# A new order of units, loads and stores for a grouped-query attention forward and backward kernel

## The chip, the cores and the metric

The kernel runs on one core of a Trainium2 chip. The metric is device time in microseconds (us), lower is better. Ratios are computed as the mean time of one kernel's fast runs over the mean of the other's fast runs of the same rounds, so they are not quite the ratio of the medians that are quoted beside them. "Span" is the length of the one profiled execution, some 1.8 to 2.2 us shorter than that execution's measured time.

## The reference

```python
B, Hq, Hkv, Sq, Sk, D = 32, 32, 4, 4, 2048, 128       # all bf16
def fwd(q, k, v):                                      # k, v repeated 8 times over the heads
    p = softmax(einsum("bhqd,bhkd->bhqk", q, k) * D ** -0.5)
    return einsum("bhqk,bhkd->bhqd", p, v)
out, vjp = jax.vjp(fwd, q, k, v)
return (out, *vjp(grad_out))                           # out, dq, dk, dv
```

Each of the 32 batches reads K and V (4 heads of 2048 rows) and writes dK and dV of the same size. Everything else is small.

## The kernel before

The program is a list of *units* written down offline as a string of four characters each: what to do, which part, where (PSUM bank, row slot or engine), which tile. Every engine works through its own units in the order of this list.

```python
SLOTS, E_TILES, DS_TILES = 20, 2, 2          # 20 row slots of 1 MB, shared by loads and outputs
PLAN = ("a000a110b120a030b040a150e400f4A0..." ...)   # [cut: 3232 units in all]

def emit(u):
    if name in ("LK", "LV"):                 # load K or V of a head pair: 1056 or 1024 KB
        for w in (slice(0, Sk), slice(Sk, n)) if b == 0 else (slice(0, n),):
            nc.sync.dma_start(out=x[:, w], in_=src[:, w])
    elif name in ("KT", "VT", "ET", "DT"):   # four transposes on TensorE into one PSUM bank
        ...
    elif name in ("O", "DQ"):                # 32 small matmuls for each half
        for c in range(8):
            for h, r in enumerate(rows):
                nc.tensor.matmul(t[name][r, :], lhsT=left[:, j, r, odd], rhs=right[:, 4 * i + j, :, odd], ...)
    elif name in ("DV", "DK"):               # two matmuls into two PSUM banks
        ...
    elif name in ("DVe", "DKe"):             # eviction of these two banks into an output slot
        copy = nc.scalar.copy if u.where == "A" else nc.vector.tensor_copy
        copy(out=heads_of(t[name[:2], "out", g])[:, :, QW * i:QW * i + QW],
             in_=t[name[:2], i, g].rearrange("p (h c) -> p h c", h=2))
    elif name in ("SV", "SK"):               # store dV or dK of a head pair: 1024 or 1056 KB
        nc.sync.dma_start(out=(dv_r if name == "SV" else dk_r)[i][b], in_=t["D" + name[1], "out", i][:, 0:n])
    # [cut: S, DP, softmax, DS, small units]

with tc.manual_schedule():
    for u in units:
        emit(u)
```

All loads and stores are issued by one engine, SP, in the order of the list. In a steady batch of about 101 units it issues LK0 SK1 SV1 LV0 SV0 LK1 SK0 LV1. One batch is 274 matmuls, each with a weight load of its own.

## Time and profile before

| before | |
|---|---|
| time, median of 4 runs | 671.61 us (671.47 to 672.95) |
| span of the profiled run | 671.1 us |
| bytes moved | 272.65 MB in 256 transfers of about 1 MB (the first four in two halves each) |
| PE, DVE, ACT busy | 91%, 85%, 85% |

The lines on which the reading rests are in the prediction below.

```profile
q8 instruction: 69, 1.13, 0.6%
...
out_dram<-row SPq DMA_DIRECT2D x64, 1024.0 KB, 20.4
```

The reader is to see that 69 packets of 16 KB are read as instructions while the kernel runs, and that a transfer that needs about 2.5 us by itself takes 20 us from issue to landing.

### The profile page before, as it was taken

How to read it: one execution, taken by the hardware profiler on the slowest of the kernel's cores; microseconds unless marked ns; L12 is line 12 of the kernel's file. 1: busy time of each engine (PE TensorE's matmuls, PEld its weight loads, DVE VectorE, ACT ScalarE, POOL GpSimd, SP SyncE). 2: the span in 40 equal slices, each digit the busy share in tenths (PEclk: the TensorE clock that was granted, in tenths of full speed). 3: DMA queues.
4: the chain of work that ended last, by engine and by line, in shares of the span. 5: the costliest groups of instructions: out<-in, count | busy, mean ns of one | idle time of the engine just before them, and what ended most of it. 6: DMA issues, size and time to landing. Idle time of an engine off the chain costs nothing.

```text
span 671.1 us, 20678 instructions
## 1 busy us (share of the span) xinstructions
PE 607.9 (91%) x8768; PEld 401.4 (60%) x8768; DVE 572.0 (85%) x736; ACT 569.6 (85%) x802; POOL 39.0 (6%) x102
## 2 busy tenths in 40 slices
PE   6998999999998999988998989988999989898993
PEld 5665566666665666655655655655655666565651
DVE  1988799999997999988888989887888979896994
ACT  4997899999997999888888989887888979886894
POOL 0000000000000000000000000000000000000000
PEclk9999999999998999999999999998999989998997
DMA  9999999999999999999999999999999999999867
GB/s 354 417 424 423 419 381 423 423 423 423 423 426 424 424 423 424 424 425 426 414 420 425 413 417 421 414 422 424 396 388 408 417 424 424 404 421 423 347 258 322
DMA packets 37533, 273.97 MB, mean 408 GB/s; under 512 B 4160, under 2 KB 4160, under 8 KB 5184
## 3 DMA queue, kind: packets, MB, share of 16 engines
q1 hardware_dynamic: 37440, 272.65, 98.2%
q8 instruction: 69, 1.13, 0.6%
q14 instruction: 24, 0.20, 0.1%
HBM read 136.31 MB, written 136.31 MB: 406 GB/s over the span
## 4 chain that ended last, share of the span: by engine, by line
DMA 50%; PE 37%; DVE 4%; ACT 4%; issue 3%; SPq 0%; POOL 0%; DVEq 0%; ACTq 0%; POOLq 0%
DMA row<-in_k_dram 50%; PE psum L241 19%; PE psum L310 8%; PE psum L288 5%; PE psum L255 5%; ACT row L316 3%; DVE vt_sb L209 2%; DVE ds_sb L303 1%; DVE row L316 0%; DVE e_sb L260 0%; ACT e_sb L264 0%; PE psum L230 0%; SPq L226 0%; ACT dt_sb L207 0%; DVE row L296 0%
## 5 line engine op out<-in xcount | busy, mean ns | idle before, releaser
L241 PE MATMUL psum<-ident,row 128*128 128x128 f32 x2048 | 290.1, 284 | 28.4 <-DMA row<-in_k_dram 21.5
L316 ACT CAST row<-psum 128x1024 bf16<-128x1024 f32 x292 | 289.2, 1023 | 30.9 <-PE psum L310 29.1
L241 PEld LDWEIGHTS psum<-ident,row 128*128 128x128 f32 x2048 | 224.7, 143 | 94.8 <-issue 32.0
L316 DVE CAST row<-psum 128x1024 bf16<-128x1024 f32 x220 | 264.9, 1217 | 5.7 <-PE psum L310 2.9
L207 ACT COPY kt_sb<-psum 128x512 f32<-128x512 f32 x190 | 110.2, 598 | 20.6 <-PE psum L241 20.4
L207 ACT COPY vt_sb<-psum 128x512 f32<-128x512 f32 x160 | 92.0, 602 | 35.3 <-PE psum L241 34.6
L303 DVE SCALAR_TENSOR_TENSOR ds_sb<-psum,delta,e_sb 128x1024 bf16<-128x1024 f32 x64 | 82.1, 1283 | 13.4 <-PE psum L255 9.0
L310 PE MATMUL psum<-ds_sb,qp_sb 32*128 32x512 bf16 x512 | 76.9, 383 | 3.4 <-ACT row L316 1.0
L260 DVE TENSOR_SCALAR_CACHE_REDUCE e_sb<-psum 128x2048 bf16<-128x2048 f32 x32 | 73.3, 2292 | 5.7 <-PE psum L255 5.7
L310 PE MATMUL psum<-e_sb,dop_sb 32*128 32x512 bf16 x512 | 68.8, 388 | 2.5 <-issue 1.0
L209 DVE COPY kt_sb<-psum 128x1024 bf16<-128x1024 bf16 x66 | 45.0, 685 | 28.4 <-PE psum L241 27.8
L209 DVE COPY vt_sb<-psum 128x1024 bf16<-128x1024 bf16 x96 | 60.7, 684 | 10.0 <-PE psum L241 9.8
L264 ACT ACTIVATE e_sb<-psum,m 128x2048 bf16<-128x2048 f32 x32 | 64.0, 2001 | 0.2 <-DVE e_sb L260 0.2
L271 POOL TENSOR_SCALAR dop_sb<-row,rinv 128x128 bf16<-128x128 bf16 x32 | 19.3, 603 | 605.3 <-DVE rinv L268 530.3
L241 PE MATMUL psum<-ident,ds_sb 128*128 128x128 f32 x256 | 41.8, 286 | 9.6 <-DVE vt_sb L209 7.0
L288 PE MATMUL psum<-row,dt_sb 128*32 128x128 bf16 x2048 | 43.5, 222 | 6.2 <-issue 5.6
L310 PEld LDWEIGHTS <-qp_sb 32*128 32x128 bf16 x512 | 19.4, 91 | 46.1 <-issue 42.6
L255 PE MATMUL psum<-vt_sb,qdt_sb 128*32 128x512 bf16 x512 | 40.7, 388 | 4.6 <-issue 4.5
L288 PEld LDWEIGHTS <-dt_sb 128*32 128x32 bf16 x2048 | 30.8, 95 | 22.0 <-issue 21.1
L241 PEld LDWEIGHTS psum<-ident,ds_sb 128*128 128x128 f32 x256 | 26.9, 140 | 27.2 <-DVE vt_sb L209 16.4
L207 ACT COPY dt_sb<-psum 128x512 f32<-128x512 f32 x63 | 38.4, 611 | 1.0 <-PE psum L241 0.9
L288 PEld LDWEIGHTS <-et_sb 128*32 128x32 bf16 x2048 | 30.4, 95 | 13.8 <-ACT et_sb L207 11.3
(29 smaller groups left out, 310.1 us busy)
## 6 DMA issues: line engine op xcount, KB each, us to landing
out_dram<-row SPq DMA_DIRECT2D x64, 1056.0 KB, 20.1
out_dram<-row SPq DMA_DIRECT2D x64, 1024.0 KB, 20.4
row<-in_k_dram SPq DMA_DIRECT2D x62, 1056.0 KB, 18.1
row<-in_v_dram SPq DMA_DIRECT2D x62, 1024.0 KB, 20.5
row<-in_v_dram SPq DMA_DIRECT2D x4, 512.0 KB, 9.4
row<-in_k_dram SPq DMA_DIRECT2D x2, 544.0 KB, 5.3
row<-in_k_dram SPq DMA_DIRECT2D x2, 512.0 KB, 4.4
```

The lines of the kernel that those rows point to most:

```text
L207: nc.scalar.copy(out=out.bitcast(FP32), in_=in_)
L209: nc.vector.tensor_copy(out=out, in_=in_.bitcast(BF16))
L241: nc.tensor.transpose(out=ps[:, P * j:P * j + P], in_=src[:, 4 * half + j, :], identity=ident32[:])
L255: nc.tensor.matmul(out[r, QW * w:QW * w + QW], lhsT=t["qdt"][:, P * side + 32 * h:P * side + 32 * h + 32], rhs=t[x, NH * i + h][:, QW * w: ...
L260: nc.vector.tensor_scalar(out=t["e"][:], in0=t["S"], scalar1=-scale, scalar2=None, op0=ALU.mult, op1=ALU.min, accum_out=t["m"][:])
L264: nc.scalar.activation(out=t["e"][:], in_=t["S"], func=ACT.Exp, bias=t["m"][:], scale=scale, accum_out=t["l"][:])
L271: nc.gpsimd.tensor_scalar(out=t["dop"][:], in0=t["go"], scalar1=t["rinv"][:], scalar2=None, op0=ALU.mult)
L288: nc.tensor.matmul(t[name][r, :], lhsT=left[:, j, r, odd], rhs=right[:, 4 * i + j, :, odd], start=(i == 0 and c == 0), stop=(i == 1 and c ...
L303: nc.vector.scalar_tensor_tensor(out=t["ds"][:, w], in0=t["DP", i], scalar=t["dl"][:], in1=t["e"][:, w], op0=ALU.subtract, op1=ALU.mult)
L310: nc.tensor.matmul(acc[:, QW * (h % 2):QW * (h % 2) + QW], lhsT=t[still][rows[h], :], rhs=t[moving][rows[h], QW * i:QW * i + QW], start=Tr ...
L316: copy(out=heads_of(t[name[:2], "out", g])[:, :, QW * i:QW * i + QW], in_=t[name[:2], i, g].rearrange("p (h c) -> p h c", h=2))
```

## The change

The intent: batch the loads and the stores (SP now issues SV0 SK0 SV1 SK1 and LK0 LV1 LK1 LV0 in a steady batch), give output slots at the first write, have the last load land earlier so that more stores lie behind it, warm the array up before the first data, and shorten the last drain with half-size stores. The whole string of units is new, with other positions of nearly all units, other PSUM banks, and other choices of ACT or DVE for the evictions.

```diff
+LAST = 31
+WARM_UP = 20
 PLAN = (
-    # [cut: 3232 units of before]
+    # [cut: 3236 units of after]
-            T[u.b]["D" + u.name[1], "out", u.part] = slots[int(u.where, 36)]
+            T[u.b]["D" + u.name[1], "out", u.part % 2] = slots[int(u.where, 36)]
-            for w in (slice(0, Sk), slice(Sk, n)) if b == 0 else (slice(0, n),):
-                nc.sync.dma_start(out=x[:, w], in_=src[:, w])
+            nc.sync.dma_start(out=x[:, 0:n], in_=src)
-            copy(out=heads_of(t[name[:2], "out", g])[:, :, QW * i:QW * i + QW],
-                 in_=t[name[:2], i, g].rearrange("p (h c) -> p h c", h=2))
+            copy(out=t[name[:2], "out", g][:, 2 * QW * i:2 * QW * i + 2 * QW], in_=t[name[:2], i, g])
+            half, g = divmod(i, 2)
+            w = (slice(0, n), slice(0, ROW // 2), slice(ROW // 2, n))[half]
+            nc.sync.dma_start(out=(...)[g][b][:, w], in_=t["D" + name[1], "out", g][:, w])
     with tc.manual_schedule():
+        for _ in range(WARM_UP):
+            nc.tensor.transpose(out=psum[:, QW * (BANKS - 1):QW * (BANKS - 1) + P], in_=ident32[:], identity=ident32[:])
```

## The prediction

> **What bounds the kernel now.** I read the page first: the busy table, the slices, the DMA part, the chain. PE is busy 91% of the span and DVE and ACT 85%, so no compute engine is full. The DMA lines are.
>
> ```profile
> DMA  9999999999999999999999999999999999999867
> GB/s 354 417 424 423 419 381 423 423 423 423 423 426 424 424 423 424 424 425 426 414 420 425 413 417 421 414 422 424 396 388 408 417 424 424 404 421 423 347 258 322
> ...
> q1 hardware_dynamic: 37440, 272.65, 98.2%
> ...
> DMA 50%; PE 37%; DVE 4%; ACT 4%; issue 3%; SPq 0%; POOL 0%; DVEq 0%; ACTq 0%; POOLq 0%
> DMA row<-in_k_dram 50%; PE psum L241 19%; PE psum L310 8%; PE psum L288 5%; PE psum L255 5%; ACT row L316 3%; DVE vt_sb L209 2%; DVE ds_sb L303 1%; DVE row L316 0%; DVE e_sb L260 0%; ACT e_sb L264 0%; PE psum L230 0%; SPq L226 0%; ACT dt_sb L207 0%; DVE row L296 0%
> ```
>
> To see here: the DMA engines are full up to slice 37, at 424 GB/s in the good slices. They move 272.65 MB; at 424 GB/s that alone is 643 us of the 671. The chain puts 50% on DMA; its PE part lies in the first 255 us, where DMA and PE are both nearly full.
>
> So the question is where the other 28 us are. The stretches view splits the span (columns: stretch, length, busy us and instructions of PE, PEld, DVE, ACT, POOL, granted clock, DMA share, GB/s):
>
> ```profile
> 0.00:34.00 34.00, 26.66 (x274) 19.96 (x275) 18.84 (x26) 22.81 (x34) 1.89 (x9) 1.00 0.96 387
> 34.00:104.00 70.00, 64.86 (x932) 42.68 (x931) 60.06 (x79) 60.16 (x84) 4.79 (x12) 0.98 1.01 411
> 104.00:248.00 144.00, 138.53 (x2040) 90.59 (x2038) 131.88 (x172) 129.64 (x185) 8.38 (x21) 0.99 1.01 424
> 248.00:328.00 80.00, 72.86 (x1084) 48.17 (x1083) 70.30 (x92) 69.23 (x99) 4.79 (x12) 1.00 1.01 424
> 328.00:472.00 144.00, 130.05 (x1907) 85.93 (x1906) 124.46 (x160) 121.97 (x174) 8.38 (x21) 0.99 1.01 419
> 472.00:624.00 152.00, 139.47 (x1979) 92.23 (x1977) 131.30 (x167) 129.86 (x185) 8.38 (x21) 0.98 1.01 412
> 624.00:664.00 40.00, 35.45 (x572) 21.85 (x568) 35.16 (x45) 35.89 (x48) 2.40 (x6) 1.00 0.76 313
> 664.00:671.10 7.10, 0.00 (x0) 0.00 (x0) 0.00 (x0) 0.00 (x0) 0.00 (x0) 0.50 0.56 231
> ```
>
> To see: three losses against 424. (a) The start: 387 in 34 us loses 34*(1-387/424) = 3.0 us. (b) Slow packets with DMA share 1.01, so no lack of work: 70*(1-411/424) = 2.1, 144*(1-419/424) = 1.7 and 152*(1-412/424) = 4.3, in sum 8.1 us. (c) The end: 40*(1-313/424) = 10.5 us, and 7.1*(1-231/424) = 3.2 us, of which 1.5 us is after the last packet (it ends at 669.55 by the packet records). In the end stretch the DMA share is 0.76, so the queue is empty: stores wait for compute. The three make 25 of the 28 us; the rest is in the rounding of 424. The queue's timeline shows it as one held-up row of eleven stores:
>
> ```profile
> 614.00 3.92 SPq L320 DMA_DIRECT2D out_dram<-row  x2
> 619.27 0.34 SPq L226 DMA_DIRECT2D row<-in_v_dram  x1
> 621.69 41.73 SPq L320 DMA_DIRECT2D out_dram<-row  x11
> ```
>
> The last load is issued at 619.3 and lands at 631.7 (landing records); eleven stores, 11*2.55 = 28 us of DMA work, then have to stretch over 38 us because batches 30 and 31 are still being computed.
>
> **What the Trainium skill says.** "DMA: Bandwidth & Descriptors", section Specifications, gives 16 DMA engines per core, a fabric ceiling of 435 GB/s and an HBM share of about 358 GB/s per core; "HBM Reference", section Specifications (TRN2), adds that a core streaming alone measures about 425 GB/s. This trace agrees with 425 (424 sustained), not with 358. So about 643 us plus the ends is a floor that no order of work can pass. The same page, section Rules for kernel authors, advises at least 1 MiB per DMA; the transfers here are 1024 and 1056 KB, so the half-size first loads and last stores are the only departures. "TensorE: Matmul & The Clock Gate", Part 1, says the array runs at half clock until about 3.4 us of activity. The start agrees: the first 16 transposes that ran together took 3.65 us (228 ns each), 16 later ones 1.90 us (119 ns).
>
> **The change part by part.**
> Bytes: none are removed. Still 256 transfers of full size, in four fewer first-load halves and four more last-store halves. Floor unchanged.
> Evictions: the strided two-head output copies become contiguous, x512 of them (ACT 1023 ns, DVE 1217 ns each); I expect at most a few tens of ns. By counts, ACT takes 345 of them (before 292) and gives up 108+28+28 copies of about 600 ns for 26 gained and 64 small ones: about -12 us of 570. DVE: -53*1.217, +108*0.685, +28*0.684, -26*0.692, +28*0.692, small ones -20: about +10 of 572. Both stay far below 640, so this is worth 0 by itself.
> Start: the first K rows come whole, so the second one lands at about 8.2 us as now and V follows it instead of coming between. The 20 warm-up transposes run from 1.6 us (identity ready) for about 20*0.228 = 4.6 us, until the first row is there, and save about 16*(228-119) = 1.7 us of PE. The first softmax can start about 3 us sooner (now 15.41). But the DMA queue is full with twelve loads (12*2.55 = 31 us) whatever PE does; worth 0 to 1 us.
> End: this is the real gain. In the new order the stores behind the last load are 11 of full size and 8 halves, 15 equivalents instead of 11. The last load therefore lands at about 631.7 - 4*2.55 = 621.5 us, and 15*2.55 = 38 us of stores lie beside the last 1.6 to 2 batches of compute (19 us of PE each: 608/32). PE needs, from the landing of the last load, about what it needs now, 631.7 to 663 = 31 us. So 38 us of DMA cover 31 us of compute plus the last eviction and half-size store. From loss (c), 12.2 us without the 1.5 us after the last packet, I keep 2 us for stores that come just in time: gain about 10 us. The halves cut the last drain from about 2.55 to 1.3 us; this is in that number.
> Middle: the slow packets of (b). By the landing records, eight transfers take 19.95 us at best and 20.4 on average. Within the good stretches a load after a store, a store after a load and two stores in a row all take 2.44 to 2.57 us by their size, so grouping by four has no turnaround to save. But slow packets are rarer when more transfers are in flight: about 10 ns excess per packet with four in flight, 6 with five, 3 with six (40 to 624 us). The new order issues four stores and two loads before a load must wait for the slot of the first of these stores, so five to six are in flight where now it is mostly four to five after 328 us. I expect about 4 of the 8 us back, with little confidence.
> Sum: 671.7 - 10 - 4 - 1 = about 656.5 us.
>
> **The rivals.**
> R1: only the end is gained and the slow packets stay. At the mean rate up to 624 us (416.4 GB/s from the stretches), 272.65/0.4164 = 655 us, plus 1.5 at the end and 2 of starvation and 0.6 between span and measured time: 659 us, 1.9% faster, "same". For it: the cause of slow packets isn't visible, and 104 to 328 us was free of them with the old order.
> R2: runs of four loads make more slow packets. In the old order the excess sits nearly all in the one place per batch where two loads follow each other (V1, K0) and the store before them. Three such places per batch could add 5 to 10 us: 664 us. Against it: the first twelve loads run in a row at 2.48 to 2.57 us each with one outlier of 3.70.
> R3: everything works and the middle runs at 424 throughout: 34 us at 387 (13.2 MB), then 259.5/0.424 = 612, plus 1.5, 2 and 0.6: 650 us.
> R4: compute becomes the bound. PE needs 19.0 us per batch, DMA 20.0. If slots given at first write make evictions wait for the landing of a store, or the moved copies make PE wait 1.5 us more per batch, the time stays at 665 to 672. PE at 138.5 of 144 us in the good stretch speaks for some risk, the DMA rate of 424 in that stretch against it.
>
> **Range and chances.** The 2% line is 658.2 us. R1 lies just above, my sum just below, R3 well below. Prediction 656.5 us, 8 in 10 between 648 and 665. Chances: faster 0.58, same 0.40, slower 0.02 (slower would need R2 and R4 together and lose the end as well).
>
> **What would show it.** In the changed profile: DMA digits of 9 to the last slice and no row of stores stretched beyond 2.6 us each (end gained); DMA share near 1 but GB/s of 410 to 419 in the middle (slow packets stay, R1, R2) or 424 (R3); the chain of waits on DMA nearly throughout. If the DMA share falls below 1 in the middle, or the output copies wait for stores in the list of waits, R4 is right and I am wrong. The start is right if the first softmax instruction begins near 12.5 us while the time gains at most 1 us from it.

## The result, and the profile after

After: 674.58 us median of 4 runs (673.12 to 675.51), before in the same rounds 671.61 us. The ratio is 1.0038 with a 95% interval of 1.0016 to 1.006: 0.4% slower, "same" by the 2% rule, and outside the predicted range of 648 to 665.

The page of the kernel after, its DMA slices, queues and chain:

```profile
DMA  8999999999999999999999999999999999999997
GB/s 363 408 420 427 407 400 415 410 424 425 424 424 423 424 424 424 423 419 416 406 394 424 424 419 419 400 407 418 408 404 408 403 414 357 423 425 354 378 395 309
...
q8 instruction: 69, 1.13, 0.6%
...
PE 43%; DMA 38%; ACT 11%; DVE 4%; issue 2%; SPq 0%; ACTq 0%; DVEq 0%
```

The end is filled as predicted: digits of 9 up to slice 39, where before had 8 and 6. But the GB/s line is lower in many other slices: by more than 3 in 17 of the 40, higher by as much in 10. The stretches view says the same (columns as in the prediction):

```profile
328.00:472.00 144.00, 135.78 (x1908) 90.06 (x1904) 125.80 (x164) 122.34 (x167) 8.43 (x21) 0.99 1.01 412
472.00:624.00 152.00, 142.24 (x2012) 93.25 (x1999) 134.45 (x176) 131.75 (x182) 8.43 (x21) 1.00 0.99 400
624.00:664.00 40.00, 37.16 (x580) 22.99 (x578) 32.80 (x41) 37.91 (x53) 2.42 (x6) 1.00 0.94 385
```

412 and 400 GB/s stand where before has 419 and 412, and 385 where before has 313. What was won at the end had been lost earlier. The chain is not on DMA nearly throughout, as the prediction wanted it: PE has 43% of it where before has 37%, DMA 38% where before has 50%. The waits of the queue that issues transfers (columns: us in total, times, longest) changed their kind. Before:

```profile
SPq L320 <- DMA out_dram<-row: 125.1, 64, 2.2
SPq L226 <- DMA out_dram<-row: 105.4, 23, 5.6
SPq L320 <- DVE row L316: 89.1, 15, 9.3
```

After:

```profile
SPq L324 <- ACT row L297: 193.9, 30, 9.2
SPq L229 <- DMA out_dram<-row: 115.2, 43, 10.6
SPq L324 <- DVE row L319: 85.3, 36, 11.3
SPq L324 <- ACT row L319: 64.1, 38, 6.6
```

Before, the queue mostly waits for landings; after, it mostly waits for an engine to fill a row (L297 is the dq or o row on ACT, L319 the output copies). And the evictions wait for stores, which never showed in before, in the waits of ACT:

```profile
ACT row L319 <- DMA out_dram<-row: 11.5, 12, 1.3
```

These are the signs that the prediction had named for its rival R4. They are true, but the experiments show that they are not the whole story.

**The view that decides.** I counted the transfers that have landed by a given time, from the trace's semaphore records: each transfer raises its semaphore sixteen times, once for each DMA engine, and it has landed at the last of the sixteen. So the count is that of the slowest engine. Halves count as half; the total is 256.

```text
landed by (us)    100   200   300   400   500   600   640
before             36    74   113   152   190   229   244
after              36    75   114   152   190   228   244
```

The two kernels land their transfers at the same pace, within one transfer, all the way to 640 us. At that point each has 12 left, about 30 us of work at 2.5 us each; before's last lands at 670.0 and after's at 671.7. So nothing that the new order does to compute, to the place of the last load or to the grouping changed the pace of the slowest engine, which decides when a transfer has landed. The question of the experiments is what sets that pace, as both are well above what 424 GB/s would give.

### The profile page after: what moved, and what is told of

Same layout as the page of the kernel before. It is cut to its first block, busy times and chain, and to the rows that moved or that the text cites. A ratio compares the mean times of both kernels' runs of the same rounds, so it can differ in the third digit from the quotient of the medians.

```text
span 672.8 us, 20669 instructions
## 1 busy us (share of the span) xinstructions
PE 624.8 (93%) x8788; PEld 413.9 (62%) x8788; DVE 580.1 (86%) x757; ACT 569.3 (85%) x781; POOL 39.2 (6%) x102
## 3 DMA queue, kind: packets, MB, share of 16 engines
q1 hardware_dynamic: 37440, 272.65, 98.7%
q8 instruction: 69, 1.13, 0.6%
## 4 chain that ended last, share of the span: by engine, by line
PE 43%; DMA 38%; ACT 11%; DVE 4%; issue 2%; SPq 0%; ACTq 0%; DVEq 0%
DMA out_dram<-row 28%; PE psum L244 21%; PE psum L313 10%; ACT row L319 6%; PE psum L291 6%; DMA row<-in_v_dram 6%; PE psum L258 5%; DMA row<-in_k_dram 5%; ACT kt_sb L212 2%; DVE row L319 2%; ACT row L297 1%; DVE vt_sb L214 1%; DVE ds_sb L306 1%; ACT vt_sb L212 1%; ACT e_sb L267 0%
## 5 line engine op out<-in xcount | busy, mean ns | idle before, releaser
L319 ACT CAST row<-psum 128x1024 bf16<-128x1024 f32 x345 | 341.0, 1027 | 43.0 <-PE psum L313 30.3
L319 DVE CAST row<-psum 128x1024 bf16<-128x1024 f32 x167 | 202.7, 1218 | 7.1 <-PE psum L313 5.5
L214 DVE COPY kt_sb<-psum 128x1024 bf16<-128x1024 bf16 x174 | 117.4, 688 | 33.8 <-PE psum L244 27.6
L313 PE MATMUL psum<-ds_sb,qp_sb 32*128 32x512 bf16 x512 | 94.2, 387 | 14.7 <-ACT row L319 10.1
L214 DVE COPY vt_sb<-psum 128x1024 bf16<-128x1024 bf16 x124 | 82.5, 686 | 11.8 <-PE psum L244 9.5
L313 PE MATMUL psum<-e_sb,dop_sb 32*128 32x512 bf16 x512 | 82.8, 381 | 5.1 <-ACT row L319 1.1
L212 ACT COPY vt_sb<-psum 128x512 f32<-128x512 f32 x132 | 75.8, 602 | 6.7 <-PE psum L244 6.5
L212 ACT COPY kt_sb<-psum 128x512 f32<-128x512 f32 x82 | 47.5, 593 | 22.0 <-PE psum L244 19.7
L313 PEld LDWEIGHTS <-dop_sb 32*128 32x128 bf16 x512 | 23.7, 91 | 41.1 <-issue 30.0
L258 PEld LDWEIGHTS <-qdt_sb 128*32 128x32 bf16 x1024 | 20.7, 95 | 27.3 <-issue 19.6
```

The lines of the kernel that those rows point to most:

```text
L212: nc.scalar.copy(out=out.bitcast(FP32), in_=in_)
L214: nc.vector.tensor_copy(out=out, in_=in_.bitcast(BF16))
L258: nc.tensor.matmul(out[r, QW * w:QW * w + QW], lhsT=t["qdt"][:, P * side + 32 * h:P * side + 32 * h + 32], rhs=t[x, NH * i + h][:, QW * w: ...
L313: nc.tensor.matmul(acc[:, QW * (h % 2):QW * (h % 2) + QW], lhsT=t[still][rows[h], :], rhs=t[moving][rows[h], QW * i:QW * i + QW], start=Tr ...
L319: copy(out=t[name[:2], "out", g][:, 2 * QW * i:2 * QW * i + 2 * QW], in_=t[name[:2], i, g])
```

## The experiments

Eighteen kernels ran. Where a median of before is given, it is of the same chip and rounds.

### Transfers alone and compute alone

Four kernels take each order apart: only its loads and stores, or all its compute with the transfers cut short from batch 4 on (512 columns; stores 512 columns throughout). All four give wrong results.

```diff
 # dma_before, dma_after [cut: the slots are set to zero first]
+            if u.name in ("LK", "LV", "SV", "SK"):
                 emit(u)
 # comp_before, comp_after
-                nc.sync.dma_start(out=x[:, 0:n], in_=src)  # comp_after; comp_before has the same cut in its loop
+                w = slice(0 if b < 4 else n - QW, n)       # and the last 512 columns of each store
+                nc.sync.dma_start(out=x[:, w], in_=src[:, w])
```

dma_before:

> The transfers of the kernel before alone, in its order and slots, without any compute (wrong results on purpose). In the profile of before one DMA engine lands each transfer up to 13 us after the first one, and late in the run the spread no longer grows: the slowest of the 16 engines seems to set 2.58 us per transfer. If that engine is slow by itself: 256*2.58 + 3 = about 663 us. If it is slow only because of what compute brings (instruction fetches, waits): about 647 us (424 GB/s all the way).

dma_after:

> The transfers of the changed kernel alone, in its order. Theory loop (a store's landing, an eviction into its slot and the next store follow each other in a circle): the order of transfers costs nothing by itself, so within 3 us of the transfers of before alone. Rival grouping (four loads in a row make slow packets): 5 us or more slower than them.

comp_before:

> The kernel before with all transfers from batch 4 on cut to 512 columns, all stores too (wrong results on purpose): what compute needs when transfers cost next to nothing. All theories: clearly below 671; from the stretch where PE was 96% busy I expect 600 to 640 us.

comp_after:

> The same cut in the changed kernel. Theory loop: compute alone is not what takes 20.8 us per batch; within 10 us of the kernel before with the same cut. Rival compute (the new order of units makes the engines themselves slower; PE busy rose from 608 to 625 us): 660 us or more, 20 us or more over the other.

Measured, beside 672.72 us for before: dma_before 647.38 us (ratio 0.9621), dma_after 649.15 (0.9653), comp_before 627.18 (0.9334), comp_after 652.41 (0.9698).

Grouping loads and stores costs the transfers alone 1.8 us, and the floor of about 647 us is real. But the new order makes compute alone 25 us slower. The busy time of PE grew by the same amount, and the weight loads wait for ACT's evictions of PSUM. First the busy line of comp_before's page, then one line of the waits of its weight loads:

```profile
PE 598.3 (96%) x8768; PEld 394.9 (63%) x8768; DVE 568.7 (91%) x736; ACT 566.2 (91%) x802; POOL 39.0 (6%) x102
```

```profile
PEld psum L241 <- ACT row L316: 10.5, 33, 0.4
```

The same two of comp_after:

```profile
PE 622.5 (96%) x8788; PEld 414.0 (64%) x8788; DVE 578.3 (89%) x757; ACT 568.1 (87%) x781; POOL 39.2 (6%) x102
```

```profile
PEld psum L245 <- ACT row L320: 28.0, 79, 0.6
```

PE is "96% busy" in both, for the same matmuls (8788 in comp_after are the 8768 plus the 20 of the warm-up). Matching every instruction record to its unit shows what the busy time hides: units whose first matmul starts 0.04 to 0.075 us after the eviction of their PSUM bank ends, having waited for it. Between batches 8 and 24 they are 6.0 per batch in comp_before and 7.9 in comp_after. Compared with the usual step from a unit of the kind before them, they come 1.85 and 2.66 us late in sum per batch. The time of a batch (here and below the mean distance between the starts of the first dq matmuls, DQ, of successive batches) is 18.9 us in comp_before and 19.8 us in comp_after, so these waits could account for 0.8 of the 0.9 us. That the bank waits make this difference is read from the records; no run took them away by themselves.

This cannot be all, though. The larger of the two bounds is 647 us for before and 652 for after, and both kernels are 22 to 24 us above it.

### What do the transfers lose when compute runs beside them?

In dma_before the landings of one transfer on its sixteen engines, from first to last, spread over 2.7 us at the most. In before the spread grows: 7.7 us at 198 us (times here are those of the first landing), 12.5 us at 400, and one engine stays about 13 us late until the last load, while the second slowest is 5 to 6 us late. A difference between these two programs that the page shows is the instruction queue q8: before has 69 such packets, dma_before none. (A smaller instruction queue, q14, has 24 packets of 0.20 MB in sum in before, and 2 in dma_before and dma_pe. No run tests it.) The next runs put a bare instruction stream beside the transfers, small matmuls on a constant, without any data in common. (Wrong results.)

```diff
 # dma_pe; dma_pe_after is the same on after's transfers with 8788 matmuls
+        for j in range(8768):
+            nc.tensor.matmul(psum[:, QW * (j % BANKS):QW * (j % BANKS) + 104], lhsT=ident[:], rhs=ident[:, 0:104], ...)
 # dma_pe_half: half as many, twice as wide
+        for j in range(4384):
+            nc.tensor.matmul(psum[:, ... + 208], lhsT=ident[:], rhs=wide[:, 0:208], ...)
```

dma_pe:

> Transfers only in the order of before (647.4 us when run alone), and beside them 8768 small matmuls without any data in common with the transfers, so that the instruction stream of TensorE is as long as in the kernel before. Wrong on purpose. Theory fetch (instruction fetches ride the same 16 engines, and each costs the engine that carries it about 1.4 us): some 60 to 70 fetches appear, the landings of one transfer spread over more than 4 us, and the time rises by 4 to 12 us, to 651 to 659. Rival (the lag comes from what the engines read and write in SBUF): 646 to 649, and the spread stays below 3 us.

Measured: 666.48 us (666.38 to 666.64), beside 671.88 for before: 19 us over the transfers alone, more than the 4 to 12 that I had expected, with 68 fetches. The spread of landings is 10.3 us at 196 us and 13.5 at 403, as in before.

dma_pe_half:

> As the run of the transfers of before beside 8768 small matmuls (666.5 us), but with 4384 matmuls of twice the columns: the same busy time of TensorE, half the instructions. Wrong on purpose. Theory fetch (what delays the transfers is that the instruction stream is read by the same 16 engines): the 19 us over the transfers alone halve, to 655 to 659, with some 34 fetches. Rival (TensorE's own reads and writes slow the transfers): 664 to 668.

Measured: 656.21 us, with 34 fetches. TensorE was busy 393.5 us, beside 411.7 in dma_pe. Half the instructions, about half the loss (8.8 of 19.1 us) at nearly the same busy time: the loss goes with the number of instructions and not with the busy time of TensorE. The weight loads halve too, so their reads alone aren't set apart by this run.

The GB/s and queue lines of dma_before:

```profile
GB/s 332 426 427 424 424 419 427 427 425 427 427 424 425 426 428 428 428 427 428 427 427 428 427 428 427 426 428 428 428 429 427 427 428 427 428 429 427 427 428 346
...
q1 hardware_dynamic: 37440, 272.65, 100.4%
```

The same of dma_pe:

```profile
GB/s 349 420 422 423 422 423 423 423 422 423 423 425 421 422 423 420 409 398 398 420 421 395 420 395 422 420 419 413 428 427 427 428 426 426 429 425 428 427 428 164
...
q1 hardware_dynamic: 37440, 272.65, 98.7%
q8 instruction: 68, 1.11, 0.6%
```

And the instruction queue of dma_pe_half:

```profile
q8 instruction: 34, 0.56, 0.3%
```

To see: a queue that takes 0.6% of the engines' time costs 3% of the kernel's. The rate dips only a little while TensorE runs (to slice 26); the last slice of dma_pe, 164 GB/s, is mostly the backlog of the late engine, which the others don't help with. In the records of before a fetch takes about 0.94 us. A data packet that starts as it ends, so presumably on the same engine, takes 0.7 to 0.85 us instead of 0.31 (66 of the 69 fetches have one): about 1.4 us of one engine for each fetch. The trace does not name the engine of a packet, so how the fetches are shared out can't be read from it.

Carrying the fetches is not all of the 19.1 us, though. The packet records give this account of the loss of the slowest engine over dma_before (the last column is what the first three leave of the measured loss, so an estimate):

```text
us, mean of 16 engines   fetches and the   other slow   slowest engine
                         packets after     packets      beyond the mean
dma_pe, 19.1             5.9               5.8          7.5
dma_pe_half, 8.8         3.0               -0.6         6.4
```

Only the first part halves with the instructions. The other slow packets come in bursts of some us and are absent in dma_pe_half, and the lag of the slowest engine hardly shrinks (its spread reaches 11.8 us there, 14.2 in dma_pe). So that an instruction stream beside the transfers costs 19 us is shown; that the fetches do it by sharing the engines is shown for about a third of it, and argued for the rest.

dma_pe_after:

> The transfers of after (649.2 us when run alone) beside 8788 small matmuls without common data. Wrong on purpose. If the fetches cost both orders the same: 666 to 671, so that after with its compute is 4 to 9 us above what its transfers and its instruction stream need together. Rival (runs of four loads or stores take the fetches better): below 662, and then the waits for slots and banks make more than 12 us of the time of after. The opposite (they take them worse): above 672, and the grouping is to blame after all, by way of the fetches.

Measured: 668.94 us (668.69 to 669.35). So the transfers and instruction streams need 666.5 us in the old order and 668.9 in the new, and before (671.6) and after (674.6) are 5.1 and 5.6 us above that. The landed count agrees:

```text
landed by (us)    100   200   300   400   500   600   640
dma_before         37    77   117   157   198   238   254
dma_pe_half        37    76   115   154   194   234   250
dma_pe             37    74   112   150   190   230   246
dma_after          37    77   117   157   197   237   253.5
dma_pe_after       37    74   112   150   189   229   245
```

From 200 us on, the lines of before and after (shown above) are those of dma_pe and dma_pe_after within two transfers, and at 640 us one or two short. The end compares best: dma_pe has all its 68 fetches by 419 us, where before has had 41 of its 69 by 400 us.

The same test in the real kernel, with three quarters of the small matmuls of O and DQ left out (wrong):

```diff
 # before_few
-            for c in range(8):
+            for c in (0, 7):
```

before_few:

> The kernel before with only 2 of the 8 groups of four small matmuls in each half of O and DQ, so 178 matmuls a batch where there were 274, and about two thirds of the instruction stream. Wrong on purpose; transfers, evictions and waits as before. Theory fetch: a third of its 19 us goes, and the time is 662 to 667. Rival (in the real kernel the fetches hide behind other work): 669 to 673, as TensorE is not what bounds before.

Measured: 666.27 us (665.64 to 667.22) beside 672.92 for before, ratio 0.9902 (0.9886 to 0.9917). Its line of the instruction queue:

```profile
q8 instruction: 45, 0.74, 0.4%
```

45 fetches in place of 69, and 6.6 us less, as a third of 19 us would have it (35% fewer matmuls). Shorter compute could help the end too; the landed count (231 at 600 us, where before has 229) shows the gain in the middle already.

### The parts of the change without its order

before_parts has the order of before with all other parts of the change: contiguous output copies, warm-up, whole first loads, half-size last stores. Its edit is the non-string part of the diff above; in the string only the units of the last stores differ.

> The code of the kernel after (contiguous output copies, warm-up transposes, first loads whole, last stores in halves) with the order of units of the kernel before. Results right. Theory order: all that the change costs comes from the order of units, so this version is no slower than before: 667 to 672, the gain being the last stores in halves. Rival: one of the other parts costs time, and this version is at 674 or above.

Measured: 671.02 us beside 671.88, ratio 0.9971 (0.994 to 1.0001), results right. The other parts cost nothing and may give 0.3%; the copies take the same time as before (medians for an eviction of DV in before and after: DVE 1215 ns in both, ACT 1017 and 1018).

### Slots whose store has not landed

The chain of after in order of time (columns: start, us, what) has a row of such lines, every 20.8 us in its middle:

```profile
416.99 13.39 DMA out_dram<-row
...
437.82 13.62 DMA out_dram<-row
```

A store lands after 13.4 us, the first output two batches later goes into its slot, and 7.4 us of compute later the next store is issued. I first took this loop for the cause of everything. Distances below are counted in units of the list, about 0.2 us each. From a store to the next use of its slot, by an output or a load, it is 51 to 72 units in steady batches of after and 86 to 170 in before, because after keeps finished outputs waiting for their group of four. The slots stand free for 370 units a batch in after, 653 in before, of 2020.

Two kernels, both with right results, exchange slots only, by changing the slot character of load and store units; nothing else moves.

after_free:

> The kernel after with output slots exchanged, so that the first output of a batch no longer takes the slot of the store that was issued 64 units earlier (it takes that of a store over 100 units earlier). Results stay right. Theory loop (a store's landing holds the first eviction of two batches later, which holds the next store: 20.8 us a lap in the chain of waits): the laps go and the time falls by 8 us or more, to 655 to 667, and the chain shows no stores one after another 20.8 us apart. Theory compute (the new order needs 19.7 us a batch of the engines alone, and the transfers 20.2): the loop is only where two nearly equal bounds meet, and the time stays within 4 us of the kernel after, 671 to 678.

Measured: 688.19 us beside 671.88, ratio 1.0221 (1.0185 to 1.0258, "unclear" by the 2% rule). The premise was wrong, which I counted only afterwards: the slot that I gave to the output had been freed 71 units before, not over 100, and the load that took the other one had 44 in place of 51. It is a test of tighter slots, not of freer ones.

before_loop:

> The kernel before with its first output of a batch moved onto the slot of the store that was issued 83 units earlier, so that the kind of loop that the chain of the kernel after shows can form; everything else as before, results right. Theory loop: it slows by 6 us or more, to 678 or above. Theory compute: before has 18.9 us of compute a batch against 20.2 of transfers, so the loop has slack, and it stays within 3 us of before, 669 to 675.

Measured: 701.9 us beside 671.88, ratio 1.0439. Only slots changed, and a good kernel lost 30 us. Its chain in order of time (columns: start, us, what):

```profile
425.70 18.48 DMA out_dram<-row
444.27 1.24 DVE row L316
...
448.60 17.66 DMA out_dram<-row
```

A store lands after 18.5 us; the DVE eviction starts with the landing; 4.3 us later the next store of the loop is on its way. A lap takes 22.9 us here, and a batch 22.3 us in the mean of batches 16 to 24, where before has 20.7. So such a loop can set the pace, and the guess of "theory compute" that 83 units leave slack was wrong.

The runs that follow try to widen the distances in after. All give right results.

after_early:

> The kernel after with each store issued directly after the unit that completes it, not in a group of four, and the slots given anew so that a store is followed in its slot by a load 92 units later at the least (51 in after) and by an output 73 at the least (63). Order of compute as in after, results right. Theory slots (the held-back stores keep slots so long that the next user waits for the landing): 5 us or more faster than after, 664 to 670, with the waits for landings gone from the vector engines. Rival (the compute order itself, with its waits for banks, holds the time up): 671 to 677.

Measured: 711.23 us. Early stores in the first batches held up loads behind them in the one queue (25 transfers landed by 100 us, where after has 36). From there to 640 us it landed 207, after 208. It says nothing about the theory.

after_slots keeps the first six batches as in after, then stores early, delays V loads and has at least 115 units behind each store:

> The compute order of after, but from batch 6 on each store issued directly after the unit that completes it, the V loads of batches 8 to 27 issued 40 units later, and slots given so that after a store at least 115 units pass before its slot is loaded or written (51 in after, 73 in the failed try; 86 in before). First batches and last batches issue as in after. Results right. Theory slots (in after the wait for landings in slots given again too soon adds to what transfers and instruction fetches need): batches 8 to 24 fall from 20.8 to 20.3 to 20.6 us each, and the time to 664 to 671. Rival (slots do not matter there; fetches and bank waits together hold the pace): 20.7 us or more a batch, and 673 to 679.

Measured: 682.7 us. Batches 8 to 16 take 20.24 us each (after: 20.73), batches 16 to 24 20.84 (20.88). But at batch 28 TensorE waits 10.3 us for a V load that had been delayed behind early stores.

after_slots2, the early stores only to batch 25:

> As after_slots, but the early stores end with batch 25 and the later V loads with batch 24, so that the last seven batches issue as in after; the hole of 10 us at the first V transposes of batch 28 should go. Results right. Theory slots: batches 8 to 16 at 20.2 to 20.4 us as in after_slots, the last seven at about 17.7 as in after, and a time of 666 to 672, 3 us or more below after. Rival (what is won in the middle is paid at the end, because transfers and fetches bound the whole): 673 to 677.

Measured: 679.36 us; batches 8 to 16 at 20.35, and a wait of 4.8 us at batch 21, where one slot distance was 73.

after_slots3, distances of at least 100 nearly everywhere:

> As after_slots2, with the early stores up to batch 26 and the later V loads up to batch 27, and slots with at least 100 units between a store and the next use of its slot from batch 10 on (73 for batches 22 to 25 in after_slots2, which waited 4.8 us at one of them). Results right. Theory slots: no hole over 3 us in TensorE after 100 us, batches 8 to 16 at 20.2 to 20.4, and a total of 667 to 672, so below after. Rival (transfers and fetches bound the whole, the accidents only show it): 673 to 678.

Measured: 684.09 us; batches 8 to 16 at 20.44, and the wait of batch 28 again (10.6 us).

after_slots4, with this load exchanged for a later one:

> As after_slots3, but the V loads of batch 28 change places with the K loads of batch 29, so that the one that TensorE waited 10.6 us for is issued some 13 us earlier. Results right. Theory slots: the hole goes, and the time is 669 to 673, 2 us or more below after. Rival (the hole only shows that transfers are behind at this point, whatever the order): a hole of 5 us or more appears elsewhere, and the time is above 676.

Measured: 680.36 us. Batches 8 to 16 at 20.29, batch 28 waits 4.1 us for another load, batch 29 2.2 us. In none of its waits of ACT or DVE does an eviction wait for a landing any more. And yet:

```text
landed by (us)    100   200   300   400   500   600   640
after              36    75   114   152   190   228   244
after_slots4       36    74   113   151   189   227   242
before_loop        36    74   112   148   184   220   234
```

This is the rival's case. With the slot waits gone, compute of batches 8 to 16 ran 0.3 to 0.5 us a batch faster (batches 16 to 24 did not), but it can only have used up loads that had been fetched ahead; no more transfers landed than in after, and later a load came late. Slots that are too tight take transfers away (before_loop lands 10 fewer by 640 us); no run shows that the slots of after did. But all four versions also moved loads and stores (after_slots2 leaves the last 42 transfers as in after, the others 18 to 32), and what part of their 5 to 10 us over after comes from that was not measured apart. No run gave after wider slots and left its loads where they were.

### The end by itself

before_tail moves the loads of the last three batches of before_parts forward by 12, 24 and 36 units.

> The order of before with all other parts of the change (671.0 us in an earlier run), and the loads of batches 29, 30 and 31 moved 12, 24 and 36 units ahead of where they were, slots given anew. Results right. If the end of before is set by the compute that follows the late last load, which is what the change set out to mend: 666 to 670. Rival (the transfers that remain and the backlog of the slowest engine set the end): 670.5 to 673.

Measured: 697.2 us. The slots given anew put one output of nearly every batch 80 to 82 units behind the store of its slot (115 at the least in before), and the loop of before_loop was back (its chain is 55% stores). before_tail2 leaves the slots alone up to batch 26:

> As before_tail, but the slots stay as in before up to batch 26, so that no store is followed in its slot by an output less than 115 units later before batch 27 (78 to 86 nearly everywhere in before_tail), and the loads of batches 30 and 31 come 15 and 30 units earlier. Results right. If before_tail was slow because of its slots: below 674, with 20.0 to 20.8 us a batch in the middle as in before_parts. If in addition the late last load sets the end of before: 666 to 670. Rival for the end (transfers left and backlog): 670.5 to 674.

Measured: 676.0 us, with 20.1 (batches 8 to 16) and 20.7 us a batch (16 to 24), so the slots had been at fault in before_tail. Its last load lands at 632.9 us, before_parts' at 638.1. The landed counts at 600 and 640 us, 230 and 245, are those of before_parts. One slot wait of 7.5 us at batch 27 spoils its end, so how much an earlier last load is worth stays unmeasured; the five microseconds there moved no transfer forward.

## Why the prediction was wrong

**What bounds the kernel: right, but half of it.** DMA is the bound and 647 us is what the transfers alone take (dma_before; 643 plus the ends had been predicted).

**The losses against 424 GB/s: the step that failed.** The prediction split 28 us into slow packets without a visible cause (b) and an end in which "the queue is empty: stores wait for compute" (c), and treated (c) as recoverable by order. Both are mostly one loss. The transfers beside a bare instruction stream lose 19.1 us without any compute to wait for, by the account above 11.6 as fetches and slow packets (mean of the engines) and 7.5 as the backlog of one late engine. The prediction also misread the landing records in (c): it put the landing of before's last load at 631.7 us by pairing sorted landings with transfers. Followed by semaphore, it is 640.1 us, because one engine is 13 us behind the first; the middle one of the sixteen is done with it at 631.0. The queue is empty for most engines, as the prediction read, and the middle one's landings come up to 8 us apart. But the slowest lands one every 2.5 to 3.2 us from there to the end, and the kernel waits for it. So the slowest engine had next to no idle time at the end that an order could win.

**"End: this is the real gain", about 10 us: the term that was mis-sized.** The mechanism half worked: the last load lands 9 us earlier (631.2 us in place of 640.1; 621.5 had been predicted), and the stretch at the end carries 385 GB/s where it carried 313. The shift is nearly the four stores that were forecast (10.2 us). But 244 transfers had landed by 640 us in both kernels. Which transfers come last does not matter when what is left for the slowest engine is the same, 12 of 2.5 us; the gain was nought in place of 10 us, and after's last 12 even took 31.7 us where before's took 30.0.

**"Middle", 4 us back from more in flight: wrong.** Between 328 and 624 us before has 7.8 transfers in flight if a landing is the last of the sixteen, and 4.5 if it is the middle one, which fits the prediction's four to five. In after they are 6.3 and 3.8: fewer, not five to six. Against a best time of 309 or 319 ns by packet size, the excess of all data packets went from 13.3 to 18.5 us of the sixteen engines' mean, up and not down. Fetches don't explain that, as both kernels have 69; of the data packets over 0.45 us, 422 in before and 700 in after, only some 66 follow a fetch.

**"Worth 0" for evictions, and "about 19 us of PE" a batch unchanged: right for the copies, wrong for the order.** The contiguous copies take the same time. But compute alone went from 627 to 652 us, with more waits for PSUM banks. It still lies 17 us below the 668.9 us that transfers and instruction stream need, so it takes mostly slack; the profile shows it as engine waits, as in R4.

**Start, 0 to 1 us: right.** The full clock is granted from 5.4 us in place of 12.0, the first softmax instruction begins at 12.16 us in place of 15.41, and 36 transfers have landed by 100 us in both kernels.

**The rivals.** R4's signs (DMA share of 0.99, evictions waiting for stores) are all there, and its 665 to 672 us is closest to the 674.6. But its cause is not what sets the total: after_slots4 removes the waits of evictions for stores and lands no more transfers, and after as a whole lies only 5.6 us above dma_pe_after. R2, that runs of loads cost 5 to 10 us by slow packets, was right in kind: the excess of the data packets is 10.4 us in dma_pe and 14.6 in dma_pe_after. In time it was too large, 1.8 us without and 2.5 with instruction streams. R1 and R3 shared the error on the end.

**The 3.0 us by which after is slower.** An account from the medians: 1.8 us come from the order of transfers alone (647.4 to 649.2), 0.7 more when instruction streams run beside them (666.5 to 668.9), 0.5 with the compute (5.1 to 5.6 us above that). The last two are below the scatter between rounds and chips (the medians of before itself lie between 671.6 and 672.9), so they are an account and not a proof.

**Where the fetches come from.** The Trainium skill, "Trainium Architecture — The Big Picture", section The software stack, says that instructions are 64 bytes long and that the runtime moves the instruction streams into the engines' instruction memory when the program is loaded. The length agrees with the traces: 8768 matmuls and 8768 weight loads of 64 bytes are 1.12 MB, dma_pe's queue q8 moved 1.11; before_few's 5696 and 5696 are 0.73, its queue moved 0.74. The time of loading doesn't agree: here the packets are read during the run, beside the data. Another page has that; see the last section.

**What stays open.** Why one engine falls so much further behind than the others, and where the bursts of slow packets come from. After shows 8 us of lag on its slowest engine at 414 us where before has 12.5 at 400, with the same count landed: the count is that of the slowest engine, so the other fifteen had carried less in after, in line with its slower packets, but why they are slower isn't known. What the 5 us between dma_pe and before are is not split up either. And whether a version with right results and fewer TensorE instructions exists: that is where the runs point, and I found none that computes the same. No version beat both kernels clearly; before_parts, 0.3% under before with an interval that touches 1, is the best of them.

## What to carry to other kernels

Before planning a new order for a kernel that looks bound by DMA, run its transfers alone, its compute alone, and its transfers beside a dummy instruction stream of the same length. The third number was the nearest to a floor here: no version with right results came within 4.5 us of dma_pe's. Count landed transfers over time rather than reading rates at the end, since a thin end may be a backlog of one engine and not a lack of work. When buffers are shared by loads and outputs, check the distance from each store to the next use of its slot against the time to land; one bad pairing cost 30 us here, and none of the wider ones that were tried gained anything.

## What the Trainium skill lacked or had wrong

- "Runtime: NRT & Kernel Launch", Instruction fetch mechanics, has the fetches: blocks of 16 KiB, read by a DMA queue of the sequencer while it runs, at a cost that is called mostly hidden. The blocks agree (69 packets of 16 KB), the cost doesn't: 68 fetches beside 272.65 MB of data went with a loss of 19.1 us on 647.4, and 34 with 8.8. No page that I found says that such fetches take time from data on the same DMA engines.
- "Trainium Architecture — The Big Picture", The software stack: instruction streams are said to be moved at load. In these runs 1.11 to 1.13 MB of them are read while a kernel of about 8,770 matmuls executes.
- "DMA: Bandwidth & Descriptors", Specifications: 358 GB/s as a core's HBM limit, without the condition that both cores of a pair stream, which the page gives only later. Transfers alone on one core ran at 424 to 429 in most slices; "HBM Reference" has the fitting number, about 425.
- "DMA: Bandwidth & Descriptors", Latency and other measured facts, says that two of the sixteen engines are usually slower and guesses at a cause in software-made descriptors. Here, on a hardware queue, one engine was up to 14.1 us late, where each transfer by itself takes 2.5 us, and only beside an instruction stream (2.7 us at the most in dma_before, 3.9 in dma_after).
